# A planned attention-and-two-MLP kernel: its planner keeps the softmax's epsilon additions apart from GpSimd's work, and its table of priorities is new

## The chip, the cores and the metric

The kernel runs on one core of a Trainium2 chip. Of that core, five engines matter here: TensorE (PE; its weight loads are shown apart as PEld), VectorE (DVE), ScalarE (ACT), GpSimd (POOL) and SyncE (SP), whose queue issues nearly all DMAs. The metric is the device time of one execution in microseconds (us).

## The reference, cut to what matters

Three stages follow each other. First comes linear attention over 4 batches, 8 heads, 576 positions and 64 columns a head: `softmax(q, over columns) @ (softmax(k, over positions)^T @ v)`, each softmax with `sum + 1e-9` as divisor. Its output, 2304 tokens of 512, goes through a SwiGLU layer with 1536 inner columns and then through a bilinear layer of the same shape:

```python
q_s = np.exp(q - q.max(-1)); q_s = q_s / (q_s.sum(-1) + 1e-09)
k_s = np.exp(k - k.max(2));  k_s = k_s / (k_s.sum(2) + 1e-09)
x = q_s @ (k_s^T @ v)                       # to 2304 x 512
x = (silu(x @ w_gate) * (x @ w_val)) @ w_out
return ((x @ w_a) * (x @ w_b)) @ w_out2
```

The six weight matrices arrive in 64 bits.

## The kernel before, in words

**Plan.** The kernel does not issue its instructions in the order in which the code names them. Each call of `add` puts one piece of work on a list, with the engine, an estimated cost, what it reads and writes and, for some pieces, a second engine that could do it (`other`). `Plan.prepare` works out a due time for each piece from what waits for it. `Plan.emit` then adds to the due time of some pieces a number from a table, `MOVES` (pairs of a piece's number and a shift in us), and `Plan.order` goes through an estimated clock: it gives each engine, whenever it is free, the ready piece that is due first, and chooses the engine where there are two. The order that comes out is emitted and is fixed: each engine runs its queue in that order, and a semaphore holds an instruction until its inputs are there.

One rule of the planner concerns a port that VectorE and GpSimd share. Each piece has a flag `port`. A piece with the flag is not begun before the port is free, and keeps it until nearly its end (`port_free = t + cost - self.PORT`). Every GpSimd piece has the flag by default; VectorE's pieces have it where the code says `port=True`.

**Weights.** Weights come as 64-bit words. `convert` loads a block of them (`wr`), and builds 32-bit floats (`a`) out of the two halves of each word by a chain of integer steps on VectorE and ScalarE: an absolute value (L565 or L563), a clamp (L570), a shift (L573), a merge of the bits (L579) and an addition (L584, on VectorE as a custom instruction, or on GpSimd). The result is split into a rounded part (ScalarE, L589) and a remainder (`pair`, line L473, on VectorE or GpSimd); both stand in `w`. So `w0_2` is what block 2 of the first layer's 12 blocks gives to TensorE, and `a0_2_0` is the same block under way. Each float is also written to memory (`wf`) for later use.

**Attention.** `attend(b, g)` computes batch b for two heads; unit u is 4b + g. The names `ut`, `tm`, `kr`, `kb`, `st`, `kx`, `kv`, `qt` and `xt` with a number are tiles of that unit. For q it takes the row maxima (L844, L847), subtracts them, exponentiates, sums the rows (L910, or in ScalarE's accumulator, L870), adds epsilon to the 9 or 10 sums (L915), inverts them (L918) and multiplies (GpSimd L921, L926, L932, or ScalarE). Unit 0 to 3 come first, since the first token tile needs them.

**MLP.** The first two of five token tiles go through the first layer block by block: `ups` (L1002, L1017: 24 matmuls a block into u), `gated` (silu on ScalarE, a product on VectorE L1031, a split into `h`) and `down` (L1044: 12 matmuls into acc). While this runs, the other blocks are converted and the other attention units are computed. From about 289 us on, three larger steps (lines L1334 to L1537) do the rest.

## Time and profile before

| what | value |
|---|---|
| median of 3 runs | 934.73 us (934.3 to 935.24) |
| profiled execution | 935.4 us, its span in the trace 933.6 us |
| mean granted clock of TensorE | 0.993 |
| busy, share of the span | PE 96%, PEld 80%, DVE 78%, ACT 58%, POOL 48% |
| moved by DMA | 121.48 MB, mean 130 GB/s |

The share of the busy time is a mean over stages that differ. The page's 40 slices show TensorE at 90% or more in every slice but the first three and the last, so a reader has to look at the first tenth of the span apart from the rest.

### The profile page before, as it was taken

How to read it: one execution, taken by the hardware profiler on the slowest of the kernel's cores; microseconds unless marked ns; L12 is line 12 of the kernel's file. 1: busy time of each engine (PE TensorE's matmuls, PEld its weight loads, DVE VectorE, ACT ScalarE, POOL GpSimd, SP SyncE). 2: the span in 40 equal slices, each digit the busy share in tenths (PEclk: the TensorE clock that was granted, in tenths of full speed). 3: DMA queues.
4: the chain of work that ended last, by engine and by line, in shares of the span. 5: the costliest groups of instructions: out<-in, count | busy, mean ns of one | idle time of the engine just before them, and what ended most of it. 6: DMA issues, size and time to landing. Idle time of an engine off the chain costs nothing.

```text
span 933.6 us, 13624 instructions
## 1 busy us (share of the span) xinstructions
PE 896.7 (96%) x4716; PEld 745.7 (80%) x4716; DVE 730.7 (78%) x1128; ACT 538.0 (58%) x970; POOL 443.5 (48%) x401
## 2 busy tenths in 40 slices
PE   4689999999999999999999999999999999999998
PEld 3467777777788788888888888788878898998986
DVE  6899997688988888988878887865687666777755
ACT  4988876566766666646564456434545573644530
POOL 5453201344444656745545443342785473665720
PEclk9979999999999999999999999999999999999999
DMA  9868775578864232242342454312312302101003
GB/s 280 260 207 268 235 232 181 167 230 263 268 216 140 80 113 80 68 123 81 93 167 93 132 162 144 113 46 69 113 58 78 103 24 68 46 24 46 23 1 113
DMA packets 108156, 121.48 MB, mean 130 GB/s; under 512 B 31928, under 2 KB 83896, under 8 KB 107960
## 3 DMA queue, kind: packets, MB, share of 16 engines
q1 hardware_dynamic: 102424, 116.55, 39.7%
q10 hardware_dynamic: 5664, 4.07, 1.4%
q8 instruction: 37, 0.61, 0.3%
q14 instruction: 31, 0.25, 0.1%
HBM read 88.60 MB, written 31.98 MB: 129 GB/s over the span
## 4 chain that ended last, share of the span: by engine, by line
PE 82%; DVE 6%; DMA 5%; ACT 2%; SPq 2%; issue 1%; POOL 1%; ACTq 0%; POOLq 0%; DVEq 0%
PE p L1334 36%; PE o L1469 9%; PE u L1017 9%; PE q L1443 7%; PE acc L1044 5%; PE o L1471 2%; PE o L1478 2%; DMA ut<-in_q_dram 2%; PE o_a L1537 2%; PE o_d L1537 2%; PE o_b L1537 2%; PE o_b L1532 1%; PE o_d L1532 1%; PE o_a L1532 1%; PE xt L951 1%
## 5 line engine op out<-in xcount | busy, mean ns | idle before, releaser
L1334 PE MATMUL p<-l2w,l2w 128*128 128x512 f32 x1512 | 361.9, 391 | 1.6 <-DVE l2w L473 0.8
L1334 PEld LDWEIGHTS p<-l2w,l2w 128*128 128x128 f32 x1512 | 280.1, 188 | 60.6 <-issue 1.9
L473 POOL TENSOR_TENSOR l2w<-raww,l2w 128x512 fp32r<-128x512 f32 x72 | 103.8, 1444 | 141.7 <-ACT l2w L480 141.6
L1017 PE MATMUL u<-xhl,w 128*128 128x512 f32 x552 | 144.3, 408 | 5.1 <-DVE w L473 3.3
L480 ACT CAST l2w<-raww 128x512 fp32r<-128x512 f32 x144 | 88.5, 622 | 74.6 <-PE p L1334 25.3
L1017 PEld LDWEIGHTS u<-xhl,w 128*128 128x128 f32 x552 | 102.9, 193 | 29.4 <-DVE w L473 4.6
L473 DVE TENSOR_TENSOR temps<-p,temps 128x512 f32<-128x512 f32 x90 | 61.9, 688 | 39.6 <-PE p L1334 35.9
L473 DVE TENSOR_TENSOR l2w<-raww,l2w 128x512 fp32r<-128x512 f32 x72 | 61.6, 860 | 24.5 <-ACT l2w L480 24.5
L1044 PE MATMUL acc<-h,w 128*128 128x512 f32 x288 | 73.5, 398 | 0.0
L1347 ACT COPY temps<-p 128x512 f32<-128x512 f32 x72 | 42.2, 587 | 54.2 <-PE p L1334 54.0
L1443 PE MATMUL q<-rest,l2w 128*128 128x256 f32 x432 | 65.5, 283 | 0.0
L473 DVE TENSOR_TENSOR sums<-o,sums 128x512 f32<-128x512 f32 x64 | 43.9, 689 | 26.4 <-PE o L1469 22.0
L1044 PEld LDWEIGHTS acc<-h,w 128*128 128x128 f32 x288 | 52.6, 188 | 11.4 <-issue 0.5
L1443 PEld LDWEIGHTS q<-rest,l2w 128*128 128x128 f32 x432 | 58.3, 192 | 0.5
L1469 PE MATMUL o<-l2w,hp 128*128 128x512 f32 x168 | 56.7, 392 | 1.2 <-DVE sums L473 1.2
L1469 PE MATMUL o<-l2w,l2w 128*128 128x512 f32 x168 | 49.5, 389 | 0.0
L473 POOL TENSOR_TENSOR raww<-raww 128x256 f32<-128x256 f32 (+1 forms) x28 | 32.1, 1148 | 22.5 <-DMA raww<-wf 14.3
L473 DVE TENSOR_TENSOR raww<-raww 128x512 f32<-128x512 f32 (+1 forms) x44 | 38.0, 865 | 2.5 <-DMA raww<-wf 2.5
L1469 PEld LDWEIGHTS o<-l2w,hp 128*128 128x128 f32 x168 | 31.1, 188 | 8.8 <-DVE sums L473 2.7
L1469 PEld LDWEIGHTS o<-l2w,l2w 128*128 128x128 f32 x168 | 31.5, 188 | 6.6
L473 POOL TENSOR_TENSOR temps<-temps 128x512 f32<-128x512 f32 x16 | 22.0, 1373 | 28.1 <-DVE temps L473 28.1
L480 ACT CAST l2w<-temps 128x512 fp32r<-128x512 f32 x36 | 22.2, 619 | 21.2 <-PE o L1469 11.7
(256 smaller groups left out, 1800.4 us busy)
## 6 DMA issues: line engine op xcount, KB each, us to landing
raww<-wf SPq DMA_DIRECT2D x36, 512.0 KB, 3.8
raww<-wf SPq DMA_DIRECT2D x36, 256.0 KB, 2.7
wf<-a SPq DMA_DIRECT2D x16, 384.0 KB, 2.6
wr<-in_moe_w_gate_dram SPq DMA_DIRECT2D x22, 256.0 KB, 4.2
wr<-in_moe_w_val_dram SPq DMA_DIRECT2D x22, 256.0 KB, 4.1
wr<-in_moe_w_out_dram SPq DMA_DIRECT2D x22, 256.0 KB, 4.4
wf<-late SPq DMA_DIRECT2D x20, 256.0 KB, 3.4
wf<-early SPq DMA_DIRECT2D x16, 256.0 KB, 7.0
```

The lines of the kernel that those rows point to most:

```text
L473: engine.tensor_tensor(out=out(), in0=x(), in1=y(), op=op)
L480: add("scalar", act_us(n), lambda: nc.scalar.copy(out=hi(), in_=src()), src_keys, [hi_key])
L1017: nc.tensor.matmul(ps()[:, 0:n], lhsT=wv[:, c, :], rhs=x()[:, xs, c, 0:n], start=(a == 0 and c == 0), stop=(a == 2 and c == KD - 1))
L1044: nc.tensor.matmul(ps()[:, 0:n], lhsT=w()[:, 4 + ws, o * P:(o + 1) * P], rhs=h()[:, hs, 0:n], start=begin, stop=end)
L1334: nc.tensor.matmul(ps()[:, 0:width], lhsT=wv(o)[:, m, ws, c, :], rhs=ops_x[o][xs][1]().rearrange("p (c n) -> p c n", c=2)[:, c, 0:width], ...
L1347: add("scalar", act_us(n), lambda: nc.scalar.copy(out=to[1]()[:, 0:n], in_=ps()[:, 0:n]), [ps], to[0] if isinstance(to[0], list) else [to[ ...
L1443: nc.tensor.matmul(ps[m]()[:, 0:256], lhsT=wv(o)[:, m, ws, c % 2, :], rhs=rest_x[xs][1]().rearrange("p (c n) -> p c n", c=KD)[:, c, :], st ...
L1469: nc.tensor.matmul(ps(), lhsT=lhs(i, hs), rhs=outs_w[i][1]()[:, ws * 512:(ws + 1) * 512], **ends)
L1471: nc.tensor.matmul(ps()[:, 0:width], lhsT=outs_w[i][1]()[:, ws * 512 + r * P:ws * 512 + (r + 1) * P], rhs=hs2[i][t][1]()[:, hs * 512:hs * ...
L1478: nc.tensor.matmul(ps()[:, o * 256:(o + 1) * 256], lhsT=outs_w[i][1]()[:, ws * 512 + at:ws * 512 + at + P], rhs=rest_h[1]()[:, (2 * i + hs ...
L1532: nc.tensor.matmul(ps()[:, 0:width], lhsT=wu()[:, at:at + P], rhs=h()[:, hs * 512:hs * 512 + width], start=first and a == 0, stop=a == 2, ...
L1537: nc.tensor.matmul(ps()[:, r * 256:(r + 1) * 256], lhsT=h()[:, hs * 512 + (2 * g + r) * P:hs * 512 + (2 * g + r + 1) * P], rhs=wu()[:, ws ...
```

## The change

Three constants of the code are touched, and the table. The planner's estimate of the time that a DMA takes after its last byte (`DMA_END`) goes from 2.1 to 1.95. The addition of epsilon to the row sums of q gets the flag `port=True`. The pair `PLACES, EARLIER` is only written with parentheses. The table `MOVES` is replaced: 1391 entries before, 1592 after; 633 pieces have an entry in both, 3 of them with the same number. The pieces and what they depend on are the same. Its entries say nothing to a reader, so two lines stand for them:

```diff
-    DMA_START, DMA_END, DMA_RATE, DMA_LANES = 1.0, 2.1, 330e3, 8
+    DMA_START, DMA_END, DMA_RATE, DMA_LANES = 1.0, 1.95, 330e3, 8
...
     MOVES = (
-        0, -24.9, 3, 28.7, 5, 6.3, 8, 19.7, 9, 18.8, 10, 1.9, 12, 4.2, 13, -2.1, 15, -65.5, 16, 11.5, 25, 10.7,
...
+        4, 7.7, 10, 51.8, 20, -4.5, 21, -14.2, 33, -50.8, 38, 3.9, 43, -7.3, 52, -3.4, 53, 4.4, 55, -0.1, 56,
...
         add("vector", 0.17, lambda: nc.vector.tensor_scalar(
             out=st()[:, 2, 0:sums], in0=st()[:, 1, 0:sums], scalar1=EPS, scalar2=None, op0=ALU.add),
-            SUMS, [(st, 2)] if rows else [st])
+            SUMS, [(st, 2)] if rows else [st], port=True)
...
-    PLACES, EARLIER = 4, 16
+    PLACES, EARLIER = (4, 16)
```

What this makes of the queues shows in their rows. (After the change a line's number is 23 higher where it stands behind the table; L848 after is L825 before, and so on.) TensorE keeps its 4508 matmuls, and their order is the same from the middle of the second token tile on; before that, attention's small matmuls move among the large ones. ScalarE has 36 loads of an activation table in place of 30; before the silu of block 5 it is 12 in place of 10.

VectorE at the start of the program, its first reductions: `st` holds the row maxima of q, `kr` the column maxima of k. Before:

```order
L473 TENSOR_TENSOR tm1_120<-ut1_98 128x2x2x64
L844 TENSOR_REDUCE st0_127<-ut0_92 128x8
L847 TENSOR_REDUCE st0_127<-rests_94 128x1
L844 TENSOR_REDUCE st1_133<-ut1_98 128x8
L847 TENSOR_REDUCE st1_133<-rests_94 128x1
L825 TENSOR_REDUCE kr0_141<-kx0_115 128x1
L825 TENSOR_REDUCE kr1_144<-kx1_122 128x1
```

After, in the same place:

```order
L496 TENSOR_TENSOR tm1_120<-ut1_98 128x2x2x64
L848 TENSOR_REDUCE kr0_128<-kx0_115 128x1
L867 TENSOR_REDUCE st0_131<-ut0_92 128x8
L848 TENSOR_REDUCE kr1_138<-kx1_122 128x1
L867 TENSOR_REDUCE st1_142<-ut1_98 128x8
L870 TENSOR_REDUCE st1_142<-rests_94 128x1
L870 TENSOR_REDUCE st0_131<-rests_94 128x1
```

The reductions of k moved ahead; to feed them, ScalarE's queue now issues both DMAs of k's last positions (`rests`) first, where the second stood behind those of q.

GpSimd's queue between the multiplications of unit 4 and the remainder of block 5, before:

```order
L926 TENSOR_TENSOR ut4_426<-ut4_426,st4_485 128x512
L932 TENSOR_TENSOR ut4_426<-ut4_426,st4_485 128x128
L805 MEMSET ut5_521 128x9
L473 TENSOR_TENSOR w0_2_591<-a0_2_0_505,w0_2_591 128x2x3x256
L840 MEMSET ut4_426 128x128
L584 TENSOR_TENSOR a0_4_0_575<-a0_4_0_575,wr0_4_0_480 128x768
L932 TENSOR_TENSOR ut5_521<-ut5_521,st5_616 128x128
```

After:

```order
L955 TENSOR_TENSOR ut4_420<-ut4_420,st4_479 128x128
L949 TENSOR_TENSOR ut4_420<-ut4_420,st4_479 128x512
L825 MEMSET ut6_716 64x64 x4
L828 MEMSET ut6_716 128x9
L607 TENSOR_TENSOR a0_5_0_755<-a0_5_0_755,wr0_5_0_628 128x768
L496 TENSOR_TENSOR w0_5_815<-a0_5_0_755,w0_5_815 128x3x256
```

The remainder of block 2 and the addition of block 4's first half left GpSimd. They stand on VectorE now; its queue over the same stretch, from unit 4's epsilon addition to unit 5's first tile, after:

```order
L938 TENSOR_SCALAR st4_479<-st4_479 128x9
L593 TENSOR_SCALAR a0_3_0_554<-a0_3_0_554 128x1536
L941 RECIPROCAL st4_479<-st4_479 128x9
L596 TENSOR_SCALAR a0_3_0_554<-a0_3_0_554 128x1536
L1054 TENSOR_TENSOR u0_0_1_1_558<-s0_0_1_570,u0_0_1_1_558 128x512
L867 TENSOR_REDUCE st5_601<-ut5_531 128x8
L870 TENSOR_REDUCE st5_601<-ut5_531 128x1
L496 TENSOR_TENSOR w0_2_587<-a0_2_0_489,w0_2_587 128x2x3x256
L496 TENSOR_TENSOR h0_0_1_603<-u0_0_1_1_558,h0_0_1_603 128x512
```

Here the subtraction into `w0_2` stands behind the product of block 1, which itself needs TensorE to have ended block 1.

## Rows read from the trace of the kernel before

**Rows 1.** The page's first part: busy time, share, instructions of each engine.

```profile
PE 896.7 (96%) x4716; PEld 745.7 (80%) x4716; DVE 730.7 (78%) x1128; ACT 538.0 (58%) x970; POOL 443.5 (48%) x401
```

**Rows 2.** Busy time by stretch: from:to, length, busy (instructions), granted clock, DMA share, GB/s.

```profile
25.00:50.00 25.00, 16.08 (x86) 11.38 (x83) 22.17 (x36) 23.59 (x47) 11.28 (x16) 0.86 0.79 246
50.00:100.00 50.00, 44.36 (x220) 34.74 (x219) 47.67 (x67) 41.50 (x87) 22.86 (x25) 0.93 0.74 239
100.00:200.00 100.00, 99.21 (x531) 78.19 (x530) 82.53 (x159) 69.65 (x112) 21.11 (x47) 1.00 0.65 204
```

**Rows 3.** Timeline of TensorE, 24 to 110 us: start, length, what, idle before and releaser.

```profile
43.78 0.44 PE L822 MATMUL kx<-ident,tm 128*128 128x128 f32 x1 [4.19 <-DVE tm L473]
...
46.45 7.35 PE L1017 MATMUL u<-xhl,w 128*128 128x512 f32 x24 [1.80 <-DVE w L473]
...
61.13 2.07 PE L1017 MATMUL u<-xhl,w 128*128 128x512 f32 x4 [1.77 <-POOL w L473]
...
82.48 4.70 PE L1017 MATMUL u<-xhl,w 128*128 128x512 f32 x20
...
93.12 0.73 PE L1017 MATMUL u<-xhl,w 128*128 128x512 f32 x2 [1.05 <-DVE w L473]
```

**Rows 4.** Timeline of VectorE, 3 to 37 us, where it sat idle.

```profile
7.10 0.69 DVE L844 TENSOR_REDUCE st<-ut 128x8 f32<-128x512 f32 x1 [1.71 <-DMA ut<-in_q_dram]
...
34.02 0.69 DVE L473 TENSOR_TENSOR xhl<-xt,xhl 128x512 fp32r<-128x512 f32 x1 [1.77 <-ACT xhl L480]
35.53 0.96 DVE L570 TENSOR_SCALAR a<-a 128x1536 f32<-128x1536 f32 x1 [0.82 <-ACT a L563]
```

**Rows 5.** Line L915, the epsilon additions: durations ns min/median/max, first and last start, forms.

```profile
L915 DVE TENSOR_SCALAR st<-st x16: 154/172/1853, 17.5 to 250.6; 128x10 f32<-128x10 f32 x12, 128x9 f32<-128x9 f32 x4
```

**Rows 6.** Groups of VectorE by shape, 0 to 120 us: busy us, mean ns | idle.

```profile
L473 DVE TENSOR_TENSOR w<-a,w 128x1536 fp32r<-128x1536 f32 x2 | 4.5, 2247 | 0.0
L584 DVE CUSTOM_DVE_ANT_0 a<-wr,a 128x1536 uint16<-128x1536 uint16 x7 | 6.8, 964 | 0.1
L570 DVE TENSOR_SCALAR a<-a 128x1536 f32<-128x1536 f32 x3 | 2.9, 951 | 0.8 <-ACT a L563 0.8
L473 DVE TENSOR_TENSOR ut<-ut,kb 128x512 f32<-128x512 f32 x4 | 2.7, 669 | 0.1
L898 DVE TENSOR_SCALAR ut<-kv,ks 64x64 f32<-64x64 f32 x9 | 2.6, 284 | 0.4
L915 DVE TENSOR_SCALAR st<-st 128x9 f32<-128x9 f32 x4 | 3.6, 908 | 0.0
L915 DVE TENSOR_SCALAR st<-st 128x10 f32<-128x10 f32 x4 | 1.9, 472 | 0.0
```

**Rows 7.** Timeline of GpSimd, 56 to 70 us.

```profile
57.43 3.64 POOL L473 TENSOR_TENSOR w<-a,w 128x1536 fp32r<-128x1536 f32 x1 [1.27 <-ACT w L589]
...
66.91 1.99 POOL L584 TENSOR_TENSOR a<-a,wr 128x768 uint32<-128x768 uint32 x1 [5.69 <-DVE a L579]
```

**Rows 8.** Timeline of VectorE, 56 to 83 us.

```profile
59.88 2.15 DVE L573 TENSOR_SCALAR a<-a 128x1536 uint32<-128x1536 uint32 x1
...
67.08 1.85 DVE L915 TENSOR_SCALAR st<-st 128x9 f32<-128x9 f32 x1
...
69.93 2.44 DVE L473 TENSOR_TENSOR w<-a,w 128x1536 fp32r<-128x1536 f32 x1
...
80.18 2.12 DVE L473 TENSOR_TENSOR w<-a,w 128x768 fp32r<-128x768 f32 x1
```

**Rows 9.** Timeline of ScalarE, 57 to 60 us: a table load and the activation behind it.

```profile
58.13 1.28 ACT L863 ACT_TABLE_LOAD   x1 [0.30 <-issue]
59.43 0.74 ACT L863 ACTIVATE ut<-ut 128x640 f32<-128x640 f32 x1
```

**Rows 10.** Busy time by short stretches, columns as in rows 2.

```profile
44.00:48.00 4.00, 2.20 (x7) 1.51 (x7) 4.00 (x4) 3.99 (x16) 2.54 (x4) 0.50 0.86 230
60.00:64.00 4.00, 2.87 (x20) 2.03 (x22) 3.96 (x3) 3.79 (x21) 1.22 (x2) 0.51 0.40 126
```

335 rows, old and new, of the table MOVES are left out of this document.

## The prediction

> **What bounds the kernel now.** The page's first part makes TensorE look like the bound, busy for 96% of the span [rows 1]. The busy times by stretch show where that is a mean over two regimes [rows 2]. From 100 us on TensorE is busy for 99.21 of 100 us at the full granted clock, and VectorE has 17 us of room in the same stretch: a better order of the other engines can win almost nothing there. Between 25 and 100 us it is the other way round. From 50 to 100 us VectorE is busy for 47.67 of 50 us and TensorE for 44.36, and the granted clock averages 0.93; from 25 to 50 us it is 16.08 of 25 for TensorE, at 0.86. So what the new order is worth is decided in the first 100 us, and by VectorE's queue.
>
> The timeline of TensorE says it more closely [rows 3]. It stands still for 4.19 us before 43.78, 1.80 before 46.45, 1.77 before 61.13 and 1.05 before 93.12. Three of these four waits end with a VectorE instruction; the third ends with a subtraction on GpSimd, the remainder of block 2's weights. The four come to 8.81 us. Block 4 starts at 82.48 without a wait, but VectorE's remainder of its second half had begun at 80.18 and run 2.12 us [rows 8], so TensorE had only about 0.2 us in hand there.
>
> What makes VectorE late is partly idleness and partly stretching. It idled 1.71 us before its first maximum of q, 1.77 before a split of x and 0.82 before a clamp that waited for ScalarE [rows 4]. And some of its instructions took far longer than their kind does. The epsilon addition has a median of 172 ns and a longest of 1853 [rows 5]. That longest one began at 67.08 and ended at 68.93; GpSimd's addition had begun at 66.91 and ended at 68.90 [rows 7, 8]. The shift at 59.88 took 2.15 us and ended at 62.03, behind GpSimd's subtraction, which ran from 57.43 to 61.07; its like, the clamp of the same shape, takes 0.95 [rows 6 to 8]. So a VectorE instruction that works from SBUF to SBUF in this way waits inside its own duration until GpSimd's instruction has ended.
>
> The Trainium skill says the same in "SBUF — State Buffer", section "SBUF: two separate sides": the port pair that the two engines share is an exclusive lock that whoever starts first holds for the whole instruction. The ends above agree with that, 0.03 us apart. But that page of the Trainium skill also names VectorE instructions with two SBUF inputs as takers of the lock, and this speaks against a change that moves such instructions to VectorE and takes epsilon additions out of their way: by that rule the sum would come out as in the first rival below.
>
> **What the change does to VectorE, term by term.** I count to the point where TensorE's start-up stalls end, block 5's weights at about 93 us. Up to there the two queues were compared piece by piece.
>
> *Added to VectorE's queue for good.* The subtraction of kb for units 1 and 3, from GpSimd: 2 x 0.67 = 1.34 us. The absolute value of block 1's first half, from ScalarE: priced as the clamp of its shape, 0.95. The same for half of block 5, half that shape: 0.5. The remainder of block 0's second matrix, a third of the 1536 shape at 2247 ns: 0.75. The remainder of block 2: 2.25. The addition for block 4's first half: 0.96. Prices are in [rows 6]. Sum 6.75 us.
>
> *Removed for good.* Three scalings of kv, to ScalarE: 3 x 0.284 = 0.85 [rows 6]. Two absolute values, to ScalarE, of a third and of half of the 1536 shape: 0.8. The custom additions of block 0's first two matrices change places with GpSimd, which costs nothing either way. Sum 1.65. Net +5.1 us of work on the engine that is the bound. Pieces that only change places on VectorE (the maxima of units 5 and 7, two products) are paid at another time and count zero over the stretch.
>
> *The epsilon additions.* Eight fall into the first 120 us: 3.6 + 1.9 = 5.5 us, where eight at the median would take 1.4 [rows 5, 6]. 4.1 us were waits. I take 2.9, since part of a wait is only passed on: behind the one at 67.08, the subtraction at 69.93 came 1.00 us after its end; without the wait of 1.68 it would have stood at the same busy port at 68.25 and waited 0.65 there [rows 8]. Bounds: 0, if the new order makes them collide all the same, and 4.1.
>
> *The shift at 59.88.* Its extra 1.2 us (2.15 less 0.95) go with GpSimd's subtraction, which is gone: -1.2. Bounds 0 and 1.2.
>
> *Idleness.* The 0.82 us before the clamp go, because VectorE now makes that absolute value itself. The 1.77 before the split of x: the splits now stand where ScalarE is ahead, and other work fills VectorE before them. I take both, 2.6; bounds 0 and 2.6. Of the 1.71 us at 7.10 the reductions of k can fill most, since the DMA of k's last positions is issued two places earlier; I take 1.3, bounds 0 and 1.7.
>
> Sum: +5.1 - 2.9 - 1.2 - 2.6 - 1.3 = -2.9 us at the end of start-up.
>
> *The collisions that stay.* Two GpSimd instructions of this stretch, 3.64 and 1.99 us long [rows 7], are gone from its queue, so there is less left to collide with; but the subtraction at 80.18, 2.12 us where the shape takes half of what the 1536 one does, collides with a GpSimd addition that is still there. I change nothing for these; bounds -2 to +2.
>
> *TensorE.* It has the same matmuls. In its queue the transposition of kr for unit 4 now stands in front of block 1, where it stood behind it, so block 1 can wait for a VectorE reduction that itself stands behind a 0.95 us absolute value. All 24 matmuls of block 1 are queued behind it. I price that at 0, since VectorE's remainder of block 1 comes earlier by more than that; without this cover it costs about 1.5 us (the 0.95 and a reduction).
>
> *ScalarE* takes over 1.65 us and two more table loads before block 5, each 1.28 us, with the activation 1.30 us after the load's start [rows 9]: 4.2 us more. It was busy for 41.50 of 50 us [rows 2], so 8.5 us of room hide it. *DMA*: SP's order of loads is the same but for copies of block 0 and 1 that go one to three places earlier; the share was 0.74, and I price it at 0.
>
> *After 100 us* TensorE has 0.8 us of idle time in 100 [rows 2], and any new order draws new small stalls while it removes old ones: -0.6, since the wait before the remainder of block 5 (1.05 us) [rows 3] should not come back in full; bounds -2 to +2.
>
> Together -3.5 us. The profiled execution's own time is 935.4, so 931.9; it lies 0.7 above the median of the runs, 934.73, and against that the same difference gives **931.2 us**.
>
> The other rule to weigh is in the Trainium skill's "ScalarE: Activation LUTs", section "What ACT_TABLE_LOAD costs": a load of about 1.28 us and a drain of about 1.38, together 2.66 a switch. The row agrees with the load and shows no drain between it and the activation. By the Trainium skill two more loads would take 5.3 us of ScalarE's room, still hidden, and the sum would stay.
>
> **The rivals.**
>
> *The wait passes on, no change.* The port stays busy, and what stood in the additions stands in the next instruction. For: the subtraction at 69.93 would have met the same GpSimd instruction. Then the addition's gain is about half, 1.5, the shift's is 0.5, and the idleness gives 2.6 of 3.9: 5.1 - 1.5 - 0.5 - 2.6 = +0.5, with -0.6 behind it: 934.6. Here too belong stalls in the 830 us behind start-up that eat a gain of 2 or 3.
>
> *VectorE is the bound and was given 5.1 us more, slower.* Everything hangs on savings of 8.0 that must be larger than 5.1. If the idleness only moves to other places, as the splits of x now wait for longer chains of unit 3, its 3.9 us are not saved: 5.1 - 2.9 - 1.2 = +1.0; with the transposition in front of block 1 uncovered, +2.5: 937.2. It turns to slower where less than five eighths of the 8.0 is saved. Against it: two long GpSimd instructions are gone.
>
> *More than counted, faster.* TensorE ran at a granted clock of 0.50 from 44 to 48 us and 0.51 from 60 to 64 us [rows 10], which is the 1.2 GHz level; both times it had stood still just before (4.19 us, 1.77 us). An order that keeps it fed has it at 2.4 GHz there, and the four stalls of 8.81 us lie open. With the epsilon saving whole (-1.2) and the collisions at their bound (-2): -6.7, 928.0.
>
> *No effect* of the flag itself is possible too (the planner's clock may be off by more than such an addition lasts); then the table decides alone, and this is inside the first two.
>
> **How the numbers follow.** Chances: forecast 0.45, wait passed on 0.22, slower 0.18, more than counted 0.15. A measurement of this kernel tells 0.2%, 1.9 us, from no change. The forecast and the last rival are faster, but for a tenth of the forecast's chance that falls short of 1.9 us: 0.56, and a little of the others, 0.58. Same: the first rival and that tenth, less what goes to either side, 0.23. Slower: 0.19. The range goes from 927.3, just under the last rival, to 936.6, short of the worst of the slower one. The forecast's own range is 929.5 to 933.
>
> **What would show it.** Right, if the changed kernel's epsilon additions in the first 100 us are near 0.2 us each; if VectorE's first reduction of k starts before 9 us; if block 1 starts before 45 us and block 4 before 80.5; and if TensorE's idle time behind 100 us stays near what it was. Wrong, if VectorE is still late at block 2 (the subtraction that it now makes itself, behind the product of block 1), if TensorE waits before the transposition of kr for unit 4, or if new waits for ScalarE's tables show. I would be wrong in size above all if the long instructions of VectorE are as many as before under other names.

## The result, and the profile after

The changed kernel takes **924.21 us** (four runs, 923.06 to 924.89), beside 934.73 for the kernel before: ratio 0.9886, interval 0.9869 to 0.9903. It is 10.5 us faster. I had forecast 931.2 and a range from 927.3; the sign was right and the size three times too small, outside the range.

The page's first part and the row of TensorE's clock, after:

```profile
PE 893.5 (97%) x4716; PEld 743.2 (81%) x4716; DVE 718.8 (78%) x1133; ACT 542.3 (59%) x975; POOL 429.9 (47%) x397
...
PEclk9999999999999999999999999999999999999999
```

Busy time by stretch, after (columns as in [rows 2]):

```profile
25.00:50.00 25.00, 17.44 (x89) 11.23 (x88) 24.29 (x37) 22.75 (x53) 10.60 (x15) 1.00 0.88 286
50.00:100.00 50.00, 48.43 (x245) 37.56 (x245) 48.93 (x78) 49.65 (x102) 12.26 (x18) 1.00 0.77 244
100.00:200.00 100.00, 98.69 (x545) 76.91 (x544) 82.69 (x167) 69.37 (x107) 26.15 (x52) 1.00 0.66 211
```

Between 50 and 100 us TensorE is busy for 48.43 us where it was 44.36, at the full clock, and GpSimd for 12.26 where it was 22.86: almost half of GpSimd's work has left this stretch.

TensorE's timeline, after, at the places of [rows 3] (block 1 starts at 44.83, block 2 at 55.63, block 4 at 74.60; the last row is block 5's wait):

```profile
43.12 0.32 PE L850 MATMUL kb<-ident,kr 128*128 128x128 f32 x1 [0.65 <-DVE kr L848]
44.83 3.03 PE L1040 MATMUL u<-xhl,w 128*128 128x512 f32 x12 [1.39 <-ACT s L1051]
...
55.63 3.06 PE L1040 MATMUL u<-xhl,w 128*128 128x512 f32 x12 [0.44 <-DVE w L496]
...
74.60 0.71 PE L1040 MATMUL u<-xhl,w 128*128 128x512 f32 x2
...
85.83 1.67 PE L1040 MATMUL u<-xhl,w 128*128 128x512 f32 x6 [0.90 <-DVE w L496]
```

The wait of 4.19 us is gone, the 1.77 before block 2 is 0.44, and block 5's 1.05 is 0.90. A wait that [rows 3] leave out is gone too; before the change it stood just ahead of block 2's:

```profile
58.72 0.63 PE L938 MATMUL qt<-ident,ut 128*128 128x128 f32 x4 [2.09 <-DVE ut L473]
```

The wait of 1.39 us before block 1 ends with ScalarE's silu of block 0, which stands behind a table load. ScalarE's timeline, after:

```profile
42.89 1.28 ACT L1051 ACT_TABLE_LOAD   x1
44.18 0.60 ACT L1051 ACTIVATE s<-u 128x512 f32<-128x512 f32 x1
```

The same matmul found in both timelines (start in us, one profiled execution each) tells where the time was won:

| | before | after | won |
|---|---|---|---|
| first matmul of block 0 | 30.16 | 25.52 | 4.6 |
| block 1 | 46.45 | 44.83 | 1.6 |
| block 2 | 61.13 | 55.63 | 5.5 |
| block 3 | 74.32 | 66.11 | 8.2 |
| block 4 | 82.48 | 74.60 | 7.9 |
| first p matmul (large steps) | 288.56 | 279.81 | 8.75 |
| end of the last matmul | 929.00 | 916.65 | 12.35 |

So some 8 us are won by the start of block 3, most of them between the starts of blocks 1 and 3 (6.6); almost nothing comes between 90 and 280 us, and 3.6 from the large steps. (These two executions are 12.35 apart, the medians 10.5. In a second profiled execution of the changed kernel, after_again below, blocks 1 to 4 start 0.7 to 0.8 us later than here, the first p matmul 3.2 later, and the last one ends 3.7 later.)

The epsilon additions, after:

```profile
L938 DVE TENSOR_SCALAR st<-st x16: 109/162/652, 15.2 to 241.3; 128x10 f32<-128x10 f32 x12, 128x9 f32<-128x9 f32 x4
```

The longest was 1853 ns [rows 5] and is 652. But they are the smaller part. Of VectorE's other long rows, these stood in the timeline before (in [rows 8] the shift at 59.88 and the subtractions at 69.93 and 80.18 belong to them):

```profile
14.04 1.37 DVE L570 TENSOR_SCALAR a<-a 128x512 f32<-128x512 f32 x1
...
46.32 2.12 DVE L565 TENSOR_SCALAR a<-wr 128x1536 uint32<-128x1536 uint32 x1
...
53.34 2.50 DVE L584 CUSTOM_DVE_ANT_0 a<-wr,a 128x3072 uint16<-128x3072 uint16 x1
```

and these are the same instructions, and block 2's remainder, after:

```profile
13.22 0.41 DVE L593 TENSOR_SCALAR a<-a 128x512 f32<-128x512 f32 x1
...
41.51 0.95 DVE L588 TENSOR_SCALAR a<-wr 128x1536 uint32<-128x1536 uint32 x1
...
48.85 1.74 DVE L607 CUSTOM_DVE_ANT_0 a<-wr,a 128x3072 uint16<-128x3072 uint16 x1
...
53.83 1.75 DVE L496 TENSOR_TENSOR w<-a,w 128x1536 fp32r<-128x1536 f32 x1
```

Each of the long ones before the change ran beside an instruction of GpSimd that reads SBUF. GpSimd's timeline before, at three of them:

```profile
13.74 1.38 POOL L473 TENSOR_TENSOR ut<-ut,kb 128x512 f32<-128x512 f32 x1
...
46.20 1.33 POOL L473 TENSOR_TENSOR w<-a,w 128x512 fp32r<-128x512 f32 x1 [1.42 <-ACT w L589]
...
79.61 1.87 POOL L584 TENSOR_TENSOR a<-a,wr 128x768 uint32<-128x768 uint32 x1 [8.02 <-DMA ut<-in_v_dram]
```

After, the clamp at 13.22 and the absolute value at 41.51 begin before GpSimd's next such instruction, and from 54.61 on GpSimd is empty for 18.18 us:

```profile
13.34 1.42 POOL L496 TENSOR_TENSOR ut<-ut,kb 128x512 f32<-128x512 f32 x1 [1.04 <-ACT kb L853]
...
41.94 1.64 POOL L496 TENSOR_TENSOR w<-a,w 128x512 fp32r<-128x512 f32 x1 [0.73 <-ACT w L612]
...
54.49 0.12 POOL L828 MEMSET ut<- 128x9 f32 x1
72.79 1.87 POOL L607 TENSOR_TENSOR a<-a,wr 128x768 uint32<-128x768 uint32 x1 [18.18 <-DVE a L602]
```

I counted this over VectorE's 116 (after: 118) instructions up to block 4's start. "Stretch" is what an instruction took beyond the shortest eighth of its operation, shape and tile names in all runs; idle time is the rows' own; "work" is the rest. (Where the shortest eighth is drawn moves the entries by up to some 0.2 us.)

| up to block 4 | before, 82.48 | after, 74.60 | difference | in the prediction |
|---|---|---|---|---|
| work | 59.75 | 63.10 | +3.4 | +5.1 |
| stretch, epsilon additions | 2.95 | 0.36 | -2.6 | -2.9 |
| stretch, shift at 59.88 | 1.21 | 0 | -1.2 | -1.2 |
| stretch, all others | 7.54 | 2.74 | **-4.8** | 0 |
| idle | 11.03 | 8.40 | -2.6 | -3.9 |
| sum | | | -7.9 | -2.9 |

Before the change 13 of these instructions were stretched by more than 0.15 us, and all 13 ran beside a tensor_tensor of GpSimd: 11.0 of the 11.7 us of stretch. After it there are six, 2.6 us, each beside one too. The idle time can be split by the same rows. The first reductions of q and k wait 1.4 us instead of 2.8, the splits of x 0.6 instead of 1.8, the clamp's 0.82 is gone, and waits under 0.15 us come to 0.7 instead of 1.4; against that stand two new waits, 0.84 us for ScalarE before a row sum and 0.81 for GpSimd before a row maximum. From 26.5 us to block 4 VectorE has no wait of more than 0.15 us.

### The profile page after: what moved, and what is told of

It reads as the page before. It is cut to its first block, busy times and chain, and to the rows that moved or that the text cites. A ratio compares the mean times of both kernels' runs of the same rounds, so it can differ in the third digit from the quotient of the medians.

```text
span 921.3 us, 13613 instructions
## 1 busy us (share of the span) xinstructions
PE 893.5 (97%) x4716; PEld 743.2 (81%) x4716; DVE 718.8 (78%) x1133; ACT 542.3 (59%) x975; POOL 429.9 (47%) x397
## 4 chain that ended last, share of the span: by engine, by line
PE 82%; DVE 7%; DMA 4%; ACT 3%; issue 2%; SPq 1%; POOL 1%; DVEq 0%; POOLq 0%; ACTq 0%
PE p L1357 37%; PE o L1492 10%; PE u L1040 8%; PE q L1466 7%; PE acc L1067 4%; PE o L1494 2%; PE o L1501 2%; PE o_d L1560 2%; PE o_b L1560 2%; PE o_a L1560 2%; PE o_a L1555 1%; PE o_d L1555 1%; PE o_b L1555 1%; DVE w L496 1%; DVE a L602 1%
## 5 line engine op out<-in xcount | busy, mean ns | idle before, releaser
L496 POOL TENSOR_TENSOR l2w<-raww,l2w 128x512 fp32r<-128x512 f32 x65 | 91.2, 1407 | 130.9 <-ACT l2w L503 130.1
L1040 PE MATMUL u<-xhl,w 128*128 128x512 f32 x552 | 142.1, 402 | 3.9 <-DVE w L496 1.6
L1040 PEld LDWEIGHTS u<-xhl,w 128*128 128x128 f32 x552 | 100.1, 188 | 28.5 <-DVE w L496 2.9
L496 DVE TENSOR_TENSOR l2w<-raww,l2w 128x512 fp32r<-128x512 f32 x79 | 71.2, 905 | 24.0 <-ACT l2w L503 23.9
L496 POOL TENSOR_TENSOR raww<-raww 128x256 f32<-128x256 f32 (+1 forms) x34 | 36.7, 1079 | 16.1 <-DVE raww L496 6.9
L672 POOL TENSOR_TENSOR late<-late 128x512 uint32<-128x512 uint32 x14 | 19.8, 1413 | 50.6 <-DVE late L667 29.7
L496 POOL TENSOR_TENSOR temps<-temps 128x512 f32<-128x512 f32 x18 | 26.4, 1468 | 27.8 <-DVE temps L496 27.6
L496 POOL TENSOR_TENSOR l2w<-temps,l2w 128x512 fp32r<-128x512 f32 x20 | 30.7, 1535 | 16.4 <-ACT l2w L503 16.2
```

The costliest lines, as they stand in the source:

```text
L496: engine.tensor_tensor(out=out(), in0=x(), in1=y(), op=op)
L672: engine.tensor_tensor(out=u32(), in0=u32(), in1=r()[..., 0], op=ALU.add)
L1040: nc.tensor.matmul(ps()[:, 0:n], lhsT=wv[:, c, :], rhs=x()[:, xs, c, 0:n], start=(a == 0 and c == 0), stop=(a == 2 and c == KD - 1))
```

## Experiments

Times are medians; ratios are to the kernel before, beside each on the same chip. My theory after the comparison: VectorE sets the pace up to block 4, and its instructions are stretched by GpSimd's. The rivals: the epsilon additions alone; k's earlier reductions; TensorE's clock; and, for the 3.6 us, that the order of the large steps has no gain of its own.

**GpSimd's empty stretch filled again.** The changed kernel with work there that nobody reads or waits for, in pool_adds additions with two SBUF inputs, in pool_sets memsets:

```
             self.ops[n]["runs"][run[n]][2]()
+            if n == 405:                      # behind unit 6's column of ones, at 54.5 us
+                self.load_gpsimd()
...
+        for _ in range(3):                    # pool_adds
+            nc.gpsimd.tensor_tensor(out=idle_work()[:, 0:1536].rearrange("p (r n) -> p r n", n=P),
+                                    in0=ident.unsqueeze(1).to_broadcast([P, 12, P]),
+                                    in1=ident.unsqueeze(1).to_broadcast([P, 12, P]), op=ALU.add)
+        for _ in range(6):                    # pool_sets
+            nc.gpsimd.memset(idle_work()[:, 0:1536], 0.0)
```

> The changed kernel with three additions of 128x1536 numbers on GpSimd that nobody reads (both inputs in SBUF, some 3.6 us each by the row of block 2's remainder), into SBUF that is free then, in its gap from 54.6 to 72.8 us. Theory that GpSimd's instructions stretch VectorE's and that this sets the start: VectorE's instructions of this stretch that go from SBUF to SBUF, all at their own length now, wait for GpSimd's; three waits of up to 3.6 us each, block 4 starts 3 to 8 us later than 74.6, and the time is 927 to 932. Rival (VectorE has room there, or only one or two instructions meet): under 1.5 us, 924 to 926.

> The same gap with six memsets of 128x1536 numbers on GpSimd (no SBUF input, some 1.5 us each, 9 us in all). If any GpSimd instruction that writes SBUF holds VectorE's up: block 4 later by 2 to 6 us, 926 to 930. If only those that also read SBUF do, or VectorE has room: within 1 us, 923.5 to 925.5.

Measured: pool_adds 931.12 (0.9970, 0.9956 to 0.9984), pool_sets 923.76 (0.9891, 0.9877 to 0.9906). Three useless additions make the kernel 7.4 us slower than memsets of the same length, which cost nothing that can be told (the changed kernel takes 924.21). GpSimd's timeline of pool_adds:

```profile
60.47 9.38 POOL L483 TENSOR_TENSOR idle_work<-ident 128x1536 f32<-128x1536 f32 x3 [5.36 <-DVE a L618]
```

VectorE's of pool_adds:

```profile
60.84 2.99 DVE L607 TENSOR_SCALAR a<-a 128x768 uint32<-128x768 uint32 x1
63.75 0.15 DVE L927 RECIPROCAL ks<-ks 128x1 f32<-128x1 f32 x1
63.86 3.38 DVE L613 SCALAR_TENSOR_TENSOR a<-wr,a 128x768 uint32<-128x768 uint32 x1
67.17 0.57 DVE L932 TENSOR_SCALAR ut<-kv,ks 64x64 f32<-64x64 f32 x2
67.77 2.89 DVE L618 CUSTOM_DVE_ANT_0 a<-wr,a 128x1536 uint16<-128x1536 uint16 x1
```

and the same three instructions in pool_sets, whose memsets run from 59.14 for 9.19 us:

```profile
59.53 1.70 DVE L605 TENSOR_SCALAR a<-a 128x768 uint32<-128x768 uint32 x1
...
61.27 0.96 DVE L611 SCALAR_TENSOR_TENSOR a<-wr,a 128x768 uint32<-128x768 uint32 x1
...
62.75 0.96 DVE L616 CUSTOM_DVE_ANT_0 a<-wr,a 128x1536 uint16<-128x1536 uint16 x1
```

Each of the three met one addition and grew from 0.55, 0.96 and 0.96 us (their lengths in the changed kernel) to 2.99, 3.38 and 2.89: 6.8 us, and block 4 starts 6.9 us later than in pool_sets (81.18, 74.24). What VectorE is stretched by reaches the end almost one to one. This shows in reverse the mechanism behind the term of 4.8 us, in one stretch of the start; that the long rows of the old order, most of them outside that stretch, were such cases is read from the timelines above. The Trainium skill's "SBUF — State Buffer", section "SBUF: two separate sides", says that a VectorE instruction with two SBUF inputs takes the lock only against a GpSimd instruction that reads SBUF; the trace agrees: beside memsets the two instructions with two inputs keep their 0.96 us, and only a tensor_scalar is held up.

**The epsilon additions alone.** Units 4 to 7 leave the addition out and take the reciprocal of the sums themselves, in the old and in the new order:

```
-        add("vector", 0.17, lambda: nc.vector.tensor_scalar(
+        add("vector", 0.17, lambda: None if rows else nc.vector.tensor_scalar(
...
-        add("vector", 0.21, lambda: nc.vector.reciprocal(out=st()[:, 3, 0:sums], in_=st()[:, 2, 0:sums]),
+        add("vector", 0.21, lambda: nc.vector.reciprocal(out=st()[:, 3, 0:sums], in_=st()[:, 1 if rows else 2, 0:sums]),
```

> The kernel before without the epsilon additions of units 4 to 7 (left out: 1e-9 added to sums of softmax that are 1 or more; the reciprocal reads the sums themselves). Two of these four took 1853 and 1444 ns. As the prediction priced them (seven tenths of each wait are won): 2.1 us of the 3.0, 932.3. Rival that the wait passes on to the next instruction at the port, or that TensorE doesn't stand still for VectorE behind these two: 0 to 0.8 us, 933.6 to 934.4.

> The changed kernel without the epsilon additions of units 4 to 7 (left out, as in before_no_eps). They take 156 to 161 ns each there and wait for nothing, 0.64 us in all. If the new order has won what these waits cost: 0 to 0.6 us, 923.6 to 924.2. Rival (VectorE's queue is still so full that what leaves it shows at more than its size): 922 to 923.

Measured: 931.94 (0.9976, 0.9968 to 0.9985) and 923.82 (0.9883, 0.9869 to 0.9897). In the old order the four are worth 2.3 us, in the new nothing that can be told: the new order has won what they cost, as priced, and the theory that they are the whole gain falls.

**The flag alone.** The kernel before with the flag and nothing else:

```
-            SUMS, [(st, 2)] if rows else [st])
+            SUMS, [(st, 2)] if rows else [st], port=True)
```

> The kernel before with the planner's flag on the epsilon additions, the old table and the old landing constant. Theory that the flag does the work: the long additions (1853, 1444, 1136 ns) come down to 0.2 us, 2 to 3 us faster, 931.5 to 932.5. Rival (the table was found for the planner without it; the flag moves other operations out of an order that was found with them, and what it wins is lost again): 934.5 to 940.

Measured: 954.84 (1.0203, 1.0179 to 1.0228), 20 us slower. The flag does what it says to the additions:

```profile
L915 DVE TENSOR_SCALAR st<-st x16: 163/166/694, 17.2 to 271.9; 128x10 f32<-128x10 f32 x12, 128x9 f32<-128x9 f32 x4
```

Those of units 4 to 7 take 163 to 166 ns now, but TensorE waits elsewhere, for block 2's weights among others:

```profile
60.77 7.59 PE L1017 MATMUL u<-xhl,w 128*128 128x512 f32 x20 [3.34 <-DVE w L473]
```

With the flag the old table's numbers give another order, in which block 4 starts 11 us later (93.72) than in the kernel before. The flag's worth can't be told apart from the table's here; the new table without the flag and the landing constant by itself were not tried.

**Block 2's remainder.** It and block 4's addition go back to GpSimd in the new order (after_back), the remainder alone does (w2_back), and in the old order both go to VectorE (before_moved). The place in the order stays:

```
-            self.ops[n]["runs"][run[n]][2]()
+            runs = self.ops[n]["runs"]
+            engine = self.MADE_BY.get(n, runs[run[n]][0])
+            next(fn for e, _, fn, _ in runs if e == engine)()
...
+    MADE_BY = {225: 'gpsimd', 302: 'gpsimd'}      # after_back; w2_back: {225: 'gpsimd'}
+    MADE_BY = {225: 'vector', 302: 'vector'}      # before_moved
```

> The changed kernel in its own order, but two operations go back to GpSimd at the same place of the order: the remainder of block 2 and the addition of block 4's first half. Theory of collisions (long GpSimd instructions stretch VectorE's, and TensorE waits for block 2's remainder): block 2 starts 3 to 5 us later than the 55.63 us of the changed kernel, the half-speed stretch behind that wait comes back, and the end comes 3 to 6 us later: 927 to 930. Rival (the gain of the start comes from k's earlier reductions and from the rest of the order): under 1 us later, 924 to 925.5. Rival that VectorE is the bound by its own work: 3.2 us of VectorE work less, 1 to 3 us faster, 921 to 923.

> The changed kernel with one operation at its old engine: block 2's remainder on GpSimd, at the same place of the order. If it is what made after_back slow: block 2 starts 2 to 2.5 us later than in the changed kernel, and the end comes 2 to 5 us later than after_again's, the more the oftener the clock falls behind that wait. Rival (block 4's addition did it): within 0.7 us of after_again.

> The kernel before in its own order, but the same two operations (remainder of block 2, addition of block 4's first half) on VectorE. Theory of collisions: the epsilon addition of 1853 ns and the shift of 2.15 us go down to 0.2 and 0.95, against 3.2 us of added work; block 2 starts up to 2 us earlier than 61.13, and the time is 1 to 3 us under 934.7. Rival (VectorE is the bound by its own work, its queue was not ordered for this): 1 to 3 us slower, 936 to 938.

> The changed kernel as it is, as the measure for w2_back on the same chip: 923 to 925.

Measured: after_back 926.43 (0.9911, 0.9896 to 0.9926), w2_back 925.90 (0.9912, 0.9892 to 0.9932), after_again, the changed kernel once more, 925.59 (0.9898, 0.9882 to 0.9915); before_moved 934.66 (0.9997, 0.9988 to 1.0006). In the profiled execution of w2_back block 2 starts at 58.51 instead of 55.63 or 56.41 and block 4 at 79.03 instead of 74.60 or 75.34, with 2.4 us more stretch and 2.2 more idle time than after_again. But the medians are only 0.3 to 2.2 us apart, with overlapping intervals: that this one move pays is not settled. In the old order both moves together give nothing, and the rows say why. The epsilon addition takes 0.18 us there and the shift 0.94, as expected, and up to block 4 (81.71) the stretch falls by 2.6 us; but the work rises by 2.2, and the subtractions behind (2.43 us at 69.40, 2.12 at 79.65) are as long as before. At block 2 the remainder takes 1.75 us on VectorE instead of GpSimd's 3.64, but unit 4's subtraction is queued behind it and starts at 59.16, where it started at 57.70. The transposition of unit 4's q stands in front of block 2 and waits for it, by way of a memset of GpSimd (59.90) that waits for it too. So the two waits of 2.09 and 1.77 us before block 2 become one of 3.83. VectorE's timeline of before_moved:

```profile
57.50 1.75 DVE L477 TENSOR_TENSOR w<-a,w 128x1536 fp32r<-128x1536 f32 x1
59.16 0.88 DVE L477 TENSOR_TENSOR ut<-ut,kb 128x512 f32<-128x512 f32 x2
```

TensorE's of before_moved:

```profile
60.19 1.08 PE L942 MATMUL qt<-ident,ut 128*128 128x128 f32 x4 [3.83 <-POOL ut L844]
60.92 2.05 PE L1021 MATMUL u<-xhl,w 128*128 128x512 f32 x4
```

**k's early reductions.** In the new order they go back behind the maxima of q, with the DMA's place (after_late_k); in the old order they come forward (before_early_k):

```
+    INSTEAD = dict(scalar=(2, 6, 5, 3, 9, 8), vector=(28, 64, 38, 39, 74, 75, 32, 68))      # after_late_k
+    INSTEAD = dict(scalar=(2, 3, 5, 6, 8, 9), vector=(28, 64, 32, 38, 68, 74, 75, 39))      # before_early_k
```

> The changed kernel with the first piece of its order put back: on VectorE the reductions of k for units 0 and 1 stand behind the four maxima of q again, and the DMA of the second half of k's last positions behind the two of q. All else in the new order. Theory that the early start is worth what TensorE has in hand at block 0's first output matmul (51.63 against 53.64): 1.5 to 2.5 us slower than the changed kernel, 925.7 to 926.7. Rival (block 1 waits for ScalarE and its own weights anyway, so that the earlier attention is hidden): within 0.7 us, 923.5 to 924.9.

> The kernel before with the changed kernel's first piece of order: VectorE's two reductions of k for units 0 and 1 among the maxima of q, and the DMAs of k's last positions ahead of q's. The prediction's price was 1.3 us; in the new order it was worth 0.9. If it is a gain by itself: 933.1 to 933.8. Rival (hidden in the old order by the 4.19 us wait for unit 4's maximum, which stands on VectorE's queue behind other work): 934.4 to 935.

Measured: 925.04 (0.9898, 0.9883 to 0.9913) and 933.83 (0.9995, 0.9986 to 1.0004). 0.8 us in the new order by the medians, 0.6 in the old, neither above what a measurement tells. In after_late_k's profile blocks 1 to 4 start 0.9 to 1.0 us later than in the changed kernel's, but those of after_again, the changed kernel itself, start 0.7 to 0.8 later too. What the early reductions are worth stays open; it is too little for the gain of the start.

**TensorE's clock.** Transpositions of the identity are put in front of waiting matmuls so that TensorE is busy there: before_fed and before_fed2 in the old order, after_back_fed in after_back's.

```
+        for _ in range(times):                                  # before_fed: 14, 6, 6; before_fed2: 14, 6, 9, 7
+            nc.tensor.transpose(bank()[:, 0:P], ident, ident)   # after_back_fed: 8, ahead of block 2 alone
```

> The kernel before, with 14 transpositions of the identity put in front of unit 4's first transposition (the wait of 4.19 us that ends at 43.78) and 6 each in front of blocks 1 and 2 (the waits of 1.80 and 1.77 us), into columns that the next instruction overwrites. They fill the waits, and the granted clock should stay at 1.00 behind them. Theory that the clock's fall is a cost of its own: two stretches of about 3.4 us at half speed go, each worth 1.7, together 2 to 3.4 us: 931 to 932.5. Rival (the fall is a symptom: TensorE then only waits longer for block 2's remainder, which GpSimd ends at 61.1 whatever TensorE does): the first is worth nothing, the second at most 1.7 and less if VectorE is late at block 3 or 4: 933 to 934.4. Fillers that outlast the wait would cost 0.2 us each.

> The kernel before with transpositions of the identity in TensorE's four waits of the middle start, this time into PSUM banks that are free then: 14 ahead of unit 4's first transposition and 6 ahead of block 1, into the bank of block 0's first sum, 9 ahead of the transposition of unit 4's q and 7 ahead of block 2, into block 2's own bank. Theory that the clock's fall is a cost of its own: the granted clock stays at 1.00 from 44 to 64 us. The first fall costs nothing, since two waits lie behind it; the second lies in front of 30 us with almost no wait, and block 2 to block 3 takes 10.5 us instead of 13.2: 2.7 us, 931.7. Rival (VectorE or ScalarE is late behind block 2 anyway): 934 to 935.

> after_back (the remainder of block 2 and block 4's addition on GpSimd again) with 8 transpositions of the identity ahead of block 2's first matmul, into columns that it overwrites, so that TensorE is busy in the wait of 2.09 us that ends at 58.09 there. In after_back the granted clock then was 0.81 and 0.77 from 56 to 64 us, block 2 started 2.46 us later than in the changed kernel and block 3 4.00 later. Theory that the clock's fall is a cost of its own: the clock stays at 1.00, block 3 starts some 2.5 us later than in the changed kernel instead of 4.0, and the end is 1.5 us earlier than after_back's 926.43: 924.9. Rival (block 3 would be late anyway, by VectorE): block 3 at 70 us, 926.4.

Measured: before_fed 935.11 (1.0011, 1.0001 to 1.0021), before_fed2 936.01 (1.0014, 1.0003 to 1.0026), after_back_fed 926.03 (0.9908, 0.9893 to 0.9923). before_fed didn't test it: its fillers waited for their PSUM bank until 43.76, when the wait was over. In before_fed2 they run in the waits. The first fall is not prevented, the second is: from 60 to 64 us, where the clock was 0.51 [rows 10], it is 1.00. Busy time by stretch of before_fed2:

```profile
44.00:48.00 4.00, 2.51 (x10) 1.89 (x9) 4.00 (x3) 3.99 (x18) 2.55 (x4) 0.57 0.83 205
...
60.00:64.00 4.00, 3.18 (x31) 2.48 (x32) 3.96 (x4) 3.46 (x20) 0.91 (x2) 1.00 0.50 155
```

But VectorE isn't earlier, and the time goes into a new wait for the scaling of unit 4's kv, which stands behind the stretched epsilon addition. TensorE's timeline of before_fed2:

```profile
69.83 1.10 PE L961 MATMUL xt<-ut 128*128 128x512 f32 x2 [2.05 <-DVE ut L907]
```

VectorE's of before_fed2:

```profile
66.78 1.83 DVE L924 TENSOR_SCALAR st<-st 128x9 f32<-128x9 f32 x1
...
68.99 0.58 DVE L907 TENSOR_SCALAR ut<-kv,ks 64x64 f32<-64x64 f32 x2
```

Block 2 to block 3 takes 12.93 us instead of 13.19, where 10.5 was expected. So in the old order the second fall was a symptom; the first was not tested there. In the new order after_again has a fall at block 1 (0.87 and 0.70 from 44 to 52 us), and block 2 starts 10.8 us behind block 1 with it as without it. The fall behind block 2 is another matter. after_back_fed's median is 0.4 us below after_back's, which tells nothing, but in its profile the clock is at 1.00 from 56 to 64 us instead of 0.81 and 0.77, and block 2 to block 4 takes 18.91 us instead of 20.51. So with VectorE earlier such a fall costs 1.6 us. (In that execution block 2 started 0.9 us later than in after_back, so that block 3 came at 69.44 instead of 70.11.)

**The large steps.** early_new and late_new mix the two tables at the steps' first operation and plan anew; start_new and steps_new make both plans and take every engine's queue from one up to the steps' first matmul and from the other behind it (the second pair's edit):

```
+        new = self.planned(self.MOVES, 1.95, True)
+        old = self.planned(self.OLD_MOVES, 2.1, False)
+        first, then = (new, old) if self.EARLY_NEW else (old, new)
+        early = [first[3][n] < first[3][turn] for n in range(len(ops))]
+        of = [first if early[n] else then for n in range(len(ops))]
```

> The changed kernel (planner's flag and landing constant included) with the table's old entries for every operation of the large steps, those that run from about 280 us on: the first 280 us are planned in the new order, the rest in the old one. The two traces lie 8.7 us apart at 280 us and 12.35 at the end, so if the two parts add up, this kernel is 8.7 us faster than before: 926.0. Rival: the new order of the large steps has no gain of its own (the difference behind 280 us comes from what the start leaves behind, or is chance), then this kernel keeps all of it: 923 to 924.5. If the two parts only work together, the old steps meet the new start badly: 929 or more.

> The counterpart: the kernel before with the new entries for the operations of the large steps alone, no flag, old landing constant. If the parts add up: 3.6 us faster than before, 931.1. Rival (no gain of its own): 934.7 within 1 us.

> Both plans are made in one kernel, and every engine's queue is taken word for word from the new plan up to the first matmul of the large steps and word for word from the old plan behind it, so that (unlike early_new, which planned anew and got an order that is in neither kernel) no third order arises. If the start's gain and the steps' gain are each a property of their own piece of order: the start's 8.75 us alone, 925.7; its first p matmul at 279.8 and 640.4 us from there to the end, as in the kernel before. Rival (the old steps need the old start): its start as good, but more than 642 us behind it, 928 or more.

> The counterpart: every engine's queue from the old plan up to the first matmul of the large steps, and from the new plan behind it. If the gain of the steps is a property of their order: 3.6 us, 930.8, with the first p matmul at 288.6 and 636.8 us behind it. Rival (that gain comes from what the start leaves behind, or both pieces were fitted to each other): 934 or more.

Measured: early_new 932.79 (0.9983, 0.9972 to 0.9994), late_new 936.20 (1.0016, 1.0007 to 1.0026), start_new 929.68 (0.9949, 0.9937 to 0.9962), steps_new 938.11 (1.0042, 1.0028 to 1.0057). By the totals the theory that the parts add up lost each time. early_new came where its last rival had it, 929 or more. start_new and steps_new came where their rivals had them: start_new's first p matmul is at 279.74, with 642.43 us behind it. late_new came where neither had it. The first two got a third order from the planner. The other two pay at the seam, where two orders meet that weren't made for each other: 1.54 us in start_new, and in steps_new

```profile
295.49 15.26 PE L1550 MATMUL p<-l2w,l2w 128*128 128x512 f32 x60 [5.26 <-ACT p L1592]
```

Behind the seam the question can be read. From the 85th p matmul to the end it is 614.43 us before and 614.53 in start_new (old steps), 610.89 after and 611.24 in steps_new (new steps). And over all runs whose queues are whole, from the first p matmul to the end it takes 640.4 to 641.4 us in the old order (six kernels) and 636.7 to 637.4 in the new (nine), whenever it begins. So at least 3 us of the steps' gain belong to their order, though neither order met the other's start without a loss. Where they lie: the old order's groups of p and o matmuls

```profile
L1334 PE MATMUL p<-l2w,l2w 128*128 128x512 f32 x1512 | 361.9, 391 | 1.6 <-DVE l2w L473 0.8 <-DVE temps L473 0.8
...
L1469 PE MATMUL o<-l2w,hp 128*128 128x512 f32 x168 | 56.7, 392 | 1.2 <-DVE sums L473 1.2
```

were idle for 1.6 and 1.2 us, the new order's for 1.1 and 0.3:

```profile
L1357 PE MATMUL p<-l2w,l2w 128*128 128x512 f32 x1512 | 361.2, 390 | 1.1 <-DVE temps L496 0.8 <-DVE l2w L496 0.3
...
L1492 PE MATMUL o<-l2w,hp 128*128 128x512 f32 x168 | 56.5, 390 | 0.3 <-DVE sums L496 0.3
```

Behind the 85th p matmul all listed idle times come to 2.3 us before and 0.6 after. Most of the rest is in matmuls that start some 0.1 us late behind the one before, 24 of them before and 12 after (2.2 us of delay against 1.1), which the groups don't list as idle.

## Why the prediction was right and wrong

**The step that failed** is the term "the collisions that stay", set to 0 with bounds of -2 to +2. They fell by 4.8 us. I had the row that shows how a collision is priced (the shift at 59.88) and applied it to two instructions, the additions and that shift, though the subtraction at 80.18 stood in the same rows with more than twice the time of its shape. I wrote that with two long GpSimd instructions gone there was less left to collide with, and still counted them only as work added to VectorE, beside those two savings, and not row by row by what GpSimd had held up there. pool_adds shows both sides: GpSimd work worth nothing costs 7.4 us.

**After 100 us** I put -0.6, bounds -2 to +2, since TensorE was idle for 0.8 us in the 100 to 200 us stretch. From 100 to 280 that held. But 3.6 us came in the large steps, whose 640 us I had not looked through: a wait of 0.84 us there and four of 0.3 to 0.6, of which two of 0.3 are left, and late starts behind them. This term too lay outside its bounds.

**Right in mechanism and near in size:** the epsilon additions (-2.9 forecast; -2.6 in VectorE's count, and 2.3 by before_no_eps for half of them) and the shift (-1.2, as forecast; not tried alone). The idleness was right in its parts: the first reductions -1.3, counted -1.5; the split and the clamp -2.6, counted -2.0. But two new waits of 1.6 us together, for ScalarE and GpSimd, stood in no term, and what k's reductions bring to the end is not shown (0.6 to 0.8 by medians, within the scatter). The added work was too high, +5.1 against +3.4, in part since the count ends at block 4, in part by the remainder of 1536 numbers: its mean of 2.25 us [rows 6] held stretched ones, and alone it takes 1.75.

**TensorE and ScalarE at 0:** unit 4's transposition does wait in front of block 1, 0.65 us for the reduction of kr, as the working feared; block 1 starts 1.6 us earlier all the same. ScalarE is busy for 49.65 of 50 us, so the room is gone, and a wait for a table does show: the 1.39 us before block 1 end with a silu that had 1.28 us of table load just before it. VectorE had no wait behind that, so it need not have cost anything; that was not tried. My list of TensorE's waits, 8.81 us, left out the 2.09 before 58.72; it makes 10.9.

**The rivals.** No change at all happened in the old order (before_moved, ratio 0.9997), where the stretch given back went into the added work; in the new order it didn't. That VectorE is the bound was right, and my sign for it wrong: it is the bound, and was given back more by the stretching than it was given to do. The rival on the other side, more than counted, went the right way and named the clock as a reason. before_fed2 shows that full speed behind block 2 alone wins nothing in the old order; its other reason, collisions, was the one, at more than twice its bound. That the clock stays up is a condition of the gain, by after_back_fed, and not its source. **What would show it:** first kr at 6.65 us, block 1 at 44.83, block 4 at 74.60 and the additions near 0.2 us (one of 0.56) came as said; that long VectorE instructions might stay under other names did not. Three signs of being wrong came as well, small: 0.44 us for VectorE at block 2, 0.65 for kr, and the table.

Open: how much block 2's remainder alone is worth in the new order (0.3 to 2.2 us by medians), what each piece of the new order gives by itself to the 4.8 us, and what the wait for the table costs.

## What to carry to other kernels

When work leaves GpSimd, price two things: what the other engine takes over, and what GpSimd's instruction had held up on VectorE; the second was the larger here. Compare every VectorE row with the shortest of its shape, and ask which GpSimd instruction ended one own length before its end (the absolute value at 46.32: 48.44 less 0.95 is 47.49, and GpSimd's subtraction ended at 47.53). A low clock or a wait of TensorE in a stretch where another engine is the bound can be worth nothing by itself: fill it once and see where the wait goes, and look again once that engine is faster. And a table of priorities belongs to the planner and to the other entries that it came with: half of the change made the kernel slower, or kept less than half of the gain.

## What the runs showed of the hardware that was not expected

The clock does not fall behind every wait of one length. The changed kernel has a wait of 1.39 us before block 1 in both profiled executions; behind it the 24 matmuls of block 1 ran at 1.00 in the one, and in after_again at 0.87 from 44 to 48 us and 0.70 from 48 to 52. The second time that it fell there, behind block 5's wait (0.58 from 88 to 92 us), it did cost. After_again's row

```profile
87.70 2.74 PE L1040 MATMUL u<-xhl,w 128*128 128x512 f32 x6 [1.98 <-DVE w L496]
```

shows the 6 matmuls of 1.67 us at 2.74. Block 6 starts 11.1 us behind this row instead of 9.6, and the first p matmul comes at 282.97 instead of 279.81. How much of the scatter of 3 to 4 us among runs of one kernel comes from such falls is not shown: the granted clocks of after_again's five runs don't follow their times (0.994 at 924.25 us, 0.998 at 925.78).

A memset of GpSimd can hold VectorE up as well, but not every instruction: in pool_sets the tensor_scalar at 59.53, with one input in SBUF, took 1.70 us instead of 0.55 and ended one own length behind the first memset (61.23 less 0.55 is 60.68; a sixth of 9.19 us from 59.14 is 60.67), while the two instructions with two inputs kept their length.
